# Elementwise instructions of 1024 columns over two PSUM banks, with token blocks of 256, in a chain of a Fourier filter and two feed-forward networks

## The chip, the cores and the metric

The kernel runs on one core of one Trainium2 chip. The time is the device time of one execution in microseconds; the median of three runs stands for a kernel, and one further execution is recorded by the hardware profiler. PE is the matrix engine, PEld its weight loads, DVE the vector engine, ACT the scalar engine, POOL the GpSimd engine and SP the engine that issues most DMAs. Each works through its own list of instructions in the order in which they stand and waits where a semaphore is not yet there.

## The reference

Three computations follow each other on 8 x 3072 tokens of 256 values. First a filter along the sequence, then a feed-forward network with 2048 hidden values and a piecewise activation, then a mixture of 8 experts with 1024 hidden values each, one expert a token:

```python
X = np.fft.rfft(x, axis=1)
y = np.fft.irfft(X * F, n=x.shape[1], axis=1)          # 8 batches

h = x @ w_in                                            # 24576 x 256 @ 256 x 2048
g = np.where(h >= 1, h, np.where(h <= -1, 0.0, (h + 1) ** 2 / 4))
x = g @ w_out

expert_idx = np.argmax(x @ w_gate, axis=1)
for e in range(8):
    h = np.maximum(x[mask] @ w1[e], 0.0)
    out[mask] = gate_w[mask, None] * (h @ w2[e])
```

## The kernel before

Every product of fp32 values is made of three fp16 products (high by high, high by low, low by high), so each operand of a matmul is first split into a high half and the low rest. For the hidden values the split takes ACT (high half, a rounding copy) and POOL or DVE (the rest).

The first network works on blocks of 512 tokens and slices of 128 hidden values; one step `n` is one slice of one block, 48 x 16 = 768 steps. A step has a first layer (`l1`): six matmuls of 512 columns into one bank of the pool `psH` (two buffers, tile `hps`). Then DVE clips it into `cl`, ACT squares `cl`, DVE takes the larger of the scaled `hps` and `cl` into `g`, ACT rounds `g` to `gh` and POOL computes `gl = g - gh`. Then comes the second layer (`l2`): twelve matmuls of 264 columns (256 outputs and 8 logits), four groups of 128 tokens by three products, into four accumulators `yps` of the pool `psY` (four buffers). `LAG` says how many steps the program puts the second layer behind the first. At the end of a block `finish` copies `yps` to `ysb`, and the routing (scale, `route1`, `route2`, `hilo`, `scatter`) sends its rows to the lists of the experts. All of that is in narrow DVE instructions of 4 to 32 columns.

The Fourier transform of batch 0 runs ahead of the loop, with its own choice of buffers (`ups`, `alt`), beside the conversion of the weights (`cv_...`). The transforms of batches 1 to 7 run beside the first network: a table of due times in half-steps (`ev`, `fire`) says at which place of the program each piece is written, and a scheduler then orders the instructions of each engine. Their DVE work that matters here is `al` and `yl` (the low rests of a split, line 319) and `xq` (line 412 with PSUM, line 419 from two SBUF tiles); POOL does `xs` and `xr`. `wsl` (line 713) is the low rest of the experts' weights.

The second network works on tiles of 256 tokens of one expert, two slices at a time: `m_l1` writes 2 x 256 columns into one bank, ACT makes `hh`, DVE makes `hl`, `m_l2` accumulates. Its first tiles start while the last block of the first network is still being routed.

Of the kernel before, what the change touches and what calls it, by code (L numbers as in the profile page):

```python
# [12 lines left out]
I32 = mybir.dt.int32  # L13
# [20 lines left out]
LA, LB, LC, SA, HB, SB_, LG = 3, 14, 9, 7.4, 59.8, 7.4, 5  # L34
LAG = 3
ROW = 260
# [92 lines left out]
def tile_kernel(ctx, tc, x, w_in, w_out, w_gate, w1, w2, cst, tab, fil, out):  # L129
# [37 lines left out]
    if True:  # L167
# [26 lines left out]
        def cv_run(f, i):  # L194
            if i == 0:
                k = fp.tile([128, 512], I32, tag="cl", name="cvk")
                a = fp.tile([128, 512], I32, tag="g", name="cva")
                cv[f] = (cv[f], k, a)
            raw, k, a = cv[f]
            lo, hi = raw[:, :, 0], raw[:, :, 1]  # L200
            if i == 0:
                V.tensor_scalar(a, hi, 0x7FFFFFF, 3, op0=ALU.bitwise_and, op1=ALU.logical_shift_left)
                V.tensor_scalar(k, hi, 0x7FFFFFFF, None, op0=ALU.bitwise_and)
            elif i == 1:
                V.scalar_tensor_tensor(a, lo, 29, a, op0=ALU.logical_shift_right, op1=ALU.bitwise_or)
            elif i == 2:
                V.scalar_tensor_tensor(a, hi, -(1 << 30), a, op0=ALU.bitwise_and, op1=ALU.bitwise_or)
            else:
                w = w32[f][:, 0:512]
                V.scalar_tensor_tensor(w, k.bitcast(F32), 1.125 * 2.0 ** -15, a.bitcast(F32), op0=ALU.is_ge, op1=ALU.mult)  # L210
                V.tensor_reduce(wmx[:, 0:2, f], w.rearrange("p (a b) -> p a b", a=2), axis=AX.X, op=ALU.max, apply_absolute_value=True)

        def cv_tr(f):
            tp = psH.tile([128, 512], F32, tag="h", name="hps")
            for k in range(2):
                PE.transpose(tp[:, k * 128:(k + 1) * 128], w32[f][:, 256 + k * 128:384 + k * 128], c[:, C_ID:C_ID + 128])
            cv[f] = tp

        def cv_ev(f):
            t = fp.tile([128, 256], F32, tag="gl", name="cvt", bufs=4)  # L220
            A.activation(t, cv[f][:, 0:256], AF.Copy)
            cv[f] = t

        def cv_lg(f):
            t = cv[f]
            lg = psH.tile([128, 512], F32, tag="h", name="hps")
            for k in range(2):
# [76 lines left out]
        cal = cpool.tile([128, 128], F32R, name="cal")  # L304
        bufs = {"gl": 4, "gh": 4, "wst": 3, "xi": 1, "xg": 1, "xr": 1, "ao": 1, "ag": 1, "al": 1}

# [24 lines left out]
        def ups(u):  # L331
            if u:
                return fps()
            pool, tag = ((psY, "y"), (psF, "f"), (psY, "y"))[ring[0] % 3]
            ring[0] += 1
            return pool.tile([128, 512], F32, tag=tag, name="fps")

# [171 lines left out]

        def l1(n):  # L510
            k, f = divmod(n, NF)
            xh, xl = xt[k]
            p = psH.tile([128, 512], F32, tag="h", name="hps")
            i = 0
            for kt in range(2):
                for w, xx in ((wih, xh), (wih, xl), (wil, xh)):
                    PE.matmul(p, lhsT=w[:, kt, f * 128:(f + 1) * 128], rhs=xx[:, kt, :], start=i == 0, stop=i == 5)  # L517
                    i += 1
            q = sq[k // 6]
# [5 lines left out]
        def act(n, pc):  # L525
# [9 lines left out]
        def l2(n):  # L535
            k, f = divmod(n, NF)
            gh, gl = g_t.pop(n)
            for j in range(4):
                if f == 0:
                    yps[j] = psY.tile([128, 512], F32, tag="y", name="yps")  # L540
                s = slice(j * 128, (j + 1) * 128)
                for i, (gg, w) in enumerate(((gh, woh), (gh, wol), (gl, woh))):
                    PE.matmul(yps[j][:, 0:WO], lhsT=gg[:, s], rhs=w[:, f, :], start=f == 0 and i == 0, stop=f == NF - 1 and i == 2)  # L543
            if f == NF - 1:
                finish(k, 2 * (n + LAG) + 1)

        fin = {}

        def finish(k, h):
            ysb = fp.tile([128, 4, WO], F32, tag="ysb", name="ysb")  # L550
            for j in range(4):
                if j % 2 == 0:
                    A.activation(ysb[:, j, :], yps[j][:, 0:WO], AF.Copy)
                else:
                    V.tensor_copy(ysb[:, j, :], yps[j][:, 0:WO])
            fin[k] = ysb
            o = FO if k < NBLK - 1 else (0, 0, 0, 0, 2, 2, 2, 6, 5)
# [163 lines left out]
        for f in range(CVS, NF):  # L721
            ev(CH + 2 * (f - CVS), lambda f=f: cv_split(f))
        ev(CH + 2 * (NF - CVS), wt.close)
        ev(-8, lambda: z_load(0))
# [116 lines left out]

        def m_l1(t, fpair):
# [4 lines left out]
            for i in range(2):  # L847
                f = 2 * fpair + i
# [6 lines left out]
            hh = fp.tile([128, 2, TT], F16, tag="gh", name="hh", bufs=4)  # L855
            hl = fp.tile([128, 2, TT], F16, tag="gl", name="hl", bufs=4)
            A.activation(hh, p, AF.Relu)  # L857
            V.scalar_tensor_tensor(hl, p, 0.0, hh, op0=ALU.max, op1=ALU.subtract)  # L858
            hq.append((t, fpair, hh, hl))

        yq = {}

        def m_l2():
            t, fpair, hh, hl = hq.pop(0)
            w = M["ws"][t % SLOTS]
            if fpair == 0:
                yq[t] = [psY.tile([128, 512], F32, tag="y", name="my") for _ in range(2)]
            for tk in range(2):
                s = slice(tk * 128, (tk + 1) * 128)
                for i in range(2):  # L870
                    f = 2 * fpair + i
                    wh = w[:, 4096 + f * D:4096 + (f + 1) * D]
                    wl = w[:, 6144 + f * D:6144 + (f + 1) * D]
                    for a, (hx, wx) in enumerate(((hh, wh), (hh, wl), (hl, wh))):
                        PE.matmul(yq[t][tk][:, 0:D], lhsT=hx[:, i, s], rhs=wx, start=fpair == 0 and i == 0 and a == 0,  # L875
                                  stop=fpair == 3 and i == 1 and a == 2)
            if fpair == 3:
                _, me = mst.pop(t)
# [3 lines left out]
                for tk in range(2):  # L882
                    o = fp.tile([128, D], F32, tag=("cl", "g")[tk], name="o")
                    if tk == 0:
# [7 lines left out]

        h = 2 * ((CK + 1) * NF + LAG) + 20
# [4 lines left out]
        h2 = 2 * (NS - 1 + LAG) + 1  # L898
        ev(h2 + 5, list2)
# [8 lines left out]
        for h in range(-40, 0):  # L908
            fire(h)
        for n in range(NS + 4 * NT0):  # L910
            if n < NS:
                pc = l1(n)
            else:
                m_l1(*divmod(n - NS, 4))
            fire(2 * n)
            if n < NS:
                act(n, pc)
            if n >= LAG:
                if n - LAG < NS:
                    l2(n - LAG)  # L920
                else:
                    m_l2()
                    if n == NS + LAG:
                        m_l2()
            fire(2 * n + 1)
        while hq:
            m_l2()
        order.close()

        def tail(a, b):  # L930
            for t in range(a, b):
                m_load(t)
                m_w(t)
            for n in range(4 * a, 4 * b):
                m_l1(*divmod(n, 4))
                if n > 4 * a:
                    m_l2()
            m_l2()

# [49 lines left out]
```

## Time and profile before

| | us |
|---|---|
| median of three runs | 3844.23 (3834.99 to 3852.2) |
| profiled execution, its own time | 3843.4 |
| span of that execution, first to last instruction | 3841.6 |
| busy in the span: PE / DVE / ACT / POOL | 3551.2 / 2622.7 / 2034.7 / 1747.7 |

A row of the view by groups has: line, engine, operation, what is written and read, shape (partitions x columns), count, then busy time in us and the mean length of one in ns, then the idle time of the engine just ahead of these instructions, with what ended it. A row of the timeline has start and length in us. A row of a stretch has the busy time of PE, PEld, DVE, ACT and POOL with the number of instructions, then PE's granted clock (a share of 2.4 GHz), the DMA share and GB/s. The ends of matmuls are modelled, so PE's busy share reads high.

### The profile page before, as it was taken

Reading aid. Unit: us, or ns where it says so; the run is one execution under the profiler, and the core shown is the slowest. Engines: PE = TensorE matmul, PEld = TensorE weight load, DVE = VectorE, ACT = ScalarE, POOL = GpSimd, SP = SyncE. Lnnn points to the kernel's source line nnn. Section 1 sums busy time; section 2 is a strip of 40 time slices with the busy share of each in tenths; the row PEclk is TensorE's granted clock in tenths of the full one; section 3 lists DMA queues with packets and bytes.
Section 4 is the critical chain, followed back from the end, with each engine's and each line's share of the span. In section 5 each row is a group of like instructions: output and inputs, shape, how many; then the busy total and the mean of one; then the engine's idle time right before and its main releaser. Section 6 shows DMA issues by size and latency. Waiting matters only on the chain. (4 is left out here: it accounts for less than half of the span.)

```text
span 3841.6 us, 70301 instructions
## 1 busy us (share of the span) xinstructions
PE 3551.2 (92%) x26082; PEld 2619.9 (68%) x26082; DVE 2622.7 (68%) x4808; ACT 2034.7 (53%) x3376; POOL 1747.7 (45%) x1538
## 2 busy tenths in 40 slices
PE   6888898999889889989999998999999999999998
PEld 4555665666656656656666666666688888888887
DVE  6688878887887888788689879877753333333332
ACT  5556565666666666666666666655532222222222
POOL 1355554555555555555555555545432222222222
PEclk8899999999999999999999999999999999999999
DMA  9344443433433343434334434310222222222221
GB/s 288 115 130 136 128 132 117 133 116 108 133 116 124 121 132 119 133 113 126 123 119 129 132 114 127 112 42 19 96 63 55 51 51 51 52 52 54 51 51 51
DMA packets 326124, 395.03 MB, mean 103 GB/s; under 512 B 164047, under 2 KB 254415, under 8 KB 325264
## 3 DMA queue, kind: packets, MB, share of 16 engines
q1 hardware_dynamic: 277152, 279.90, 25.6%
q0 software_dynamic: 48624, 110.58, 9.6%
q8 instruction: 207, 3.39, 0.4%
q14 instruction: 141, 1.16, 0.1%
HBM read 439.70 MB, written 120.49 MB: 146 GB/s over the span
## 5 line engine op out<-in xcount | busy, mean ns | idle before, releaser
L532 POOL TENSOR_TENSOR gl<-g,gh 128x512 f16<-128x512 f32 x768 | 925.8, 1212 | 865.0 <-ACT gh L531 810.5
L522 ACT ACTIVATE cl<-cl,sq 128x512 f32<-128x512 f32 x768 | 622.2, 811 | 398.8 <-DVE cl L521 277.7
L528 DVE SCALAR_TENSOR_TENSOR g<-hps,sq,cl 128x512 f32<-128x512 f32 x768 | 571.9, 745 | 313.2 <-ACT cl L522 290.7
L543 PE MATMUL yps<-woh,gh 128*128 128x264 f16 x3072 | 758.5, 279 | 23.4 <-ACT gh L531 12.0
L543 PE MATMUL yps<-wol,gh 128*128 128x264 f16 x3072 | 759.4, 278 | 0.0
L543 PEld LDWEIGHTS <-gh 128*128 128x128 f16 x6144 | 596.4, 99 | 233.7 <-issue 25.6
L517 PE MATMUL hps<-xh,wih 128*128 128x512 f16 x1536 | 592.0, 386 | 136.2 <-DVE g L528 128.9
L858 DVE SCALAR_TENSOR_TENSOR hl<-mh,hh 128x512 f16<-128x512 f32 x388 | 268.2, 691 | 632.8 <-ACT hh L857 632.7
L531 ACT ACTIVATE gh<-g 128x512 f16<-128x512 f32 x768 | 479.5, 626 | 401.6 <-DVE g L528 339.6
L521 DVE TENSOR_SCALAR cl<-hps,sq 128x512 f32<-128x512 f32 x768 | 614.1, 800 | 56.8 <-PE hps L517 52.7
L857 ACT ACTIVATE hh<-mh 128x512 f16<-128x512 f32 x388 | 231.4, 597 | 723.8 <-PE mh L852 721.4
L517 PE MATMUL hps<-xl,wih 128*128 128x512 f16 x1536 | 591.4, 385 | 2.7 <-DVE xl L505 2.7
L517 PE MATMUL hps<-xh,wil 128*128 128x512 f16 x1536 | 591.1, 385 | 0.0
L543 PE MATMUL yps<-woh,gl 128*128 128x264 f16 x3072 | 540.9, 278 | 37.3 <-POOL gl L532 36.1
L852 PE MATMUL mh<-xt,wslot 128*128 128x256 f16 x4656 | 571.5, 273 | 0.0
L517 PEld LDWEIGHTS <-wih 128*128 128x128 f16 x3072 | 293.5, 99 | 382.2 <-issue 181.0
L875 PE MATMUL my<-wslot,hh 128*128 128x256 f16 x3104 | 529.1, 273 | 0.0
L852 PEld LDWEIGHTS <-wslot 128*128 128x128 f16 x4656 | 455.5, 98 | 52.9
L888 POOL DMA_INDIRECT out_dram<-o,me x194 | 191.7, 988 | 659.0 <-ACT o L885 540.4
L875 PE MATMUL my<-wslot,hl 128*128 128x256 f16 x1552 | 422.9, 273 | 0.0
L543 PEld LDWEIGHTS <-gl 128*128 128x128 f16 x3072 | 285.6, 98 | 143.2 <-POOL gl L532 63.3
L875 PEld LDWEIGHTS <-hh 128*128 128x128 f16 x3104 | 303.6, 98 | 35.1
(187 smaller groups left out, 4308.0 us busy)
## 6 DMA issues: line engine op xcount, KB each, us to landing
tf<-in_fil_dram SPq DMA_DIRECT2D x113, 512.0 KB, 3.7
tt<-in_tab_dram POOLq DMA_DIRECT2D x112, 448.0 KB, 4.3
wst<-in_w_dram SPq DMA_DIRECT2D x128, 256.0 KB, 4.3
xi<-in_x_dram SPq DMA_DIRECT2D x48, 512.0 KB, 4.3
scr<-ao SPq DMA_DIRECT2D x48, 512.0 KB, 2.9
a<-scr SPq DMA_DIRECT2D x128, 192.0 KB, 2.6
scr<-z SPq DMA_DIRECT2D x128, 192.0 KB, 3.4
zt<-scr SPq DMA_DIRECT2D x48, 512.0 KB, 4.6
```

Of the source, the lines that this page charges most:

```text
L517: PE.matmul(p, lhsT=w[:, kt, f * 128:(f + 1) * 128], rhs=xx[:, kt, :], start=i == 0, stop=i == 5)
L521: V.tensor_scalar(cl, p, q[:, 5:6], q[:, 3:4], op0=ALU.max, op1=ALU.min)
L522: A.activation(cl, cl, AF.Square, bias=q[:, 11:12], scale=q[:, 4:5])
L528: V.scalar_tensor_tensor(g, p, q[:, 7:8], cl, op0=ALU.mult, op1=ALU.max)
L531: A.activation(gh, g, AF.Copy)
L532: G.tensor_tensor(gl, g, gh, op=ALU.subtract)
L543: PE.matmul(yps[j][:, 0:WO], lhsT=gg[:, s], rhs=w[:, f, :], start=f == 0 and i == 0, stop=f == NF - 1 and i == 2)
L852: PE.matmul(p[:, i, :], lhsT=w[:, wo + kt * FE + f * 128:wo + kt * FE + f * 128 + 128], rhs=xt_[:, xo + kt, :], start=a == 0, stop=a == 5)
L857: A.activation(hh, p, AF.Relu)
L858: V.scalar_tensor_tensor(hl, p, 0.0, hh, op0=ALU.max, op1=ALU.subtract)
L875: PE.matmul(yq[t][tk][:, 0:D], lhsT=hx[:, i, s], rhs=wx, start=fpair == 0 and i == 0 and a == 0, stop=fpair == 3 and i == 1 and a == 2)
L888: G.indirect_dma_start(out=out, out_offset=IOA(ap=me.bitcast(I32)[:, tk, 1:2], axis=0), in_=o, in_offset=None, bounds_check=NTOK - 1, oob_ ...
```

## The change

The step becomes a unit of four slices (`UF = 4`) of 256 tokens: 384 units in the first network, 1024 columns each. `psH` keeps two buffers, now of 1024 columns, two banks each; `psY` goes from four to two buffers, so half a block has its two accumulators at a time. The tile `g` goes away: the second DVE instruction writes back into `cl`, which has three buffers. `gh` and `gl` have three buffers of 1024 columns instead of four of 512. `LAG` goes from 3 steps to 2 units. The second layer runs over all products with `gh` first and those with `gl` last. In the second network a unit is four slices as well, two units a tile. In the transform of batch 0 the pool `psH` takes the place of every second use of `psY`. The events keep their half-steps, with four events a unit.

```diff
-LAG = 3
+LAG = 2
+UF = 4
...
-    psY = ctx.enter_context(tc.tile_pool(name="psY", bufs=4, space=bass.MemoryType.PSUM))
+    psY = ctx.enter_context(tc.tile_pool(name="psY", bufs=2, space=bass.MemoryType.PSUM))
...
-            pool, tag = ((psY, "y"), (psF, "f"), (psY, "y"))[ring[0] % 3]
+            pool, tag = ((psY, "y"), (psF, "f"), (psH, "h"))[ring[0] % 3]
...
+        def l1(n, part, p=None):
+            k, half, f0 = unit(n)
             xh, xl = xt[k]
...
+            s = slice(half * TT, (half + 1) * TT)
+            if p is None:
+                p = psH.tile([128, UF, TT], F32, tag="h", name="hps")
+            for i in range(2 * part, 2 * part + 2):
+                f = f0 + i
+                a = 0
+                for kt in range(2):
+                    for w, xx in ((wih, xh), (wih, xl), (wil, xh)):
+                        PE.matmul(p[:, i, :], lhsT=w[:, kt, f * 128:(f + 1) * 128], rhs=xx[:, kt, s], start=a == 0, stop=a == 5)
+                        a += 1
+            return p
...
-            cl = fp.tile([128, BLK], F32, tag="cl", name="cl")
+            cl = fp.tile([128, UF, TT], F32, tag="cl", name="cl", bufs=3)
             V.tensor_scalar(cl, p, q[:, 5:6], q[:, 3:4], op0=ALU.max, op1=ALU.min)
             A.activation(cl, cl, AF.Square, bias=q[:, 11:12], scale=q[:, 4:5])
...
-            g = fp.tile([128, BLK], F32, tag="g", name="g")
-            V.scalar_tensor_tensor(g, p, q[:, 7:8], cl, op0=ALU.mult, op1=ALU.max)
-            gh = fp.tile([128, BLK], F16, tag="gh", name="gh", bufs=4)
-            gl = fp.tile([128, BLK], F16, tag="gl", name="gl", bufs=4)
-            A.activation(gh, g, AF.Copy)
-            G.tensor_tensor(gl, g, gh, op=ALU.subtract)
+            V.scalar_tensor_tensor(cl, p, q[:, 7:8], cl, op0=ALU.mult, op1=ALU.max)
+            gh = fp.tile([128, UF, TT], F16, tag="gh", name="gh", bufs=3)
+            gl = fp.tile([128, UF, TT], F16, tag="gl", name="gl", bufs=3)
+            A.activation(gh, cl, AF.Copy)
+            G.tensor_tensor(gl, cl, gh, op=ALU.subtract)
...
+            todo = [(j, i, gh, w, w is woh) for j in range(2) for i in range(UF) for w in (woh, wol)]
+            todo += [(j, i, gl, woh, False) for j in range(2) for i in range(UF)]
+            for j, i, gg, w, first in todo[12 * part:12 * part + 12]:
...
-            pool, tag = ((psH, "h"), (psF, "f"))[fpair % 2]
-            p = pool.tile([128, 2, TT], F32, tag=tag, name="mh")
+                p = psH.tile([128, UF, TT], F32, tag="h", name="mh")
```

On DVE, in the part where a transform runs beside the first network, these rows stand before (line 521 is the clip, 528 the second instruction, `al` and `xq` belong to the transform, `posi` to the routing):

```order
1927 L641 TENSOR_REDUCE pos<-t 128x4
1928 L601 MEMSET oh 128x4
1929 L642 CAST posi<-pos 128x4
1930 L319 TENSOR_TENSOR al<-a_15443,ag 96x512
1931 L412 TENSOR_TENSOR xq<-fps,tf 128x512
1932 L521 TENSOR_SCALAR cl<-hps,sq 128x512
1933 L528 SCALAR_TENSOR_TENSOR g<-hps,sq,cl 128x512
1934 L713 SCALAR_TENSOR_TENSOR wsl<-wst,wsc_c,wsh 128x512
1935 L419 TENSOR_TENSOR xq<-xq,xs 128x512
1936 L528 SCALAR_TENSOR_TENSOR g<-hps,sq,cl 128x512
```

and these in the change (line 535 is the clip, 541 the second instruction, 320, 415 and 422 are the old 319, 412 and 419):

```order
1704 L508 SCALAR_TENSOR_TENSOR xl<-fps,sq,xh 128x512
1705 L535 TENSOR_SCALAR cl<-hps,sq 128x1024
1706 L541 SCALAR_TENSOR_TENSOR cl<-hps,sq,cl 128x1024
1707 L320 TENSOR_TENSOR al<-a_16610,ag 96x512
1708 L415 TENSOR_TENSOR xq<-fps,tf 128x512
1709 L422 TENSOR_TENSOR xq<-xq,xs 128x512
1710 L535 TENSOR_SCALAR cl<-hps,sq 128x1024
1711 L320 TENSOR_TENSOR yl<-xq,yh 128x512
1712 L541 SCALAR_TENSOR_TENSOR cl<-hps,sq,cl 128x1024
```

Half as many pairs of twice the width stand among the same pieces of the transform. Of the 768 pairs before, 238 have no other instruction between clip and second instruction, of the 384 pairs of the change 110.

On POOL, from the first to the second part of one transform, before (`gl` of the first network, `xr` and `xs` of the transform, `rows` the scatter of the routing):

```order
665 L319 TENSOR_TENSOR xr<-xi,xg 128x1024
666 L532 TENSOR_TENSOR gl<-g,gh 128x512 x2
667 L319 TENSOR_TENSOR xr<-xi,xg 128x1024
668 L532 TENSOR_TENSOR gl<-g,gh 128x512 x6
669 L656 DMA rows<-row,posi 198912x260
670 L532 TENSOR_TENSOR gl<-g,gh 128x512
671 L656 DMA rows<-row,posi 198912x260
672 L532 TENSOR_TENSOR gl<-g,gh 128x512
```

and in the change:

```order
415 L320 TENSOR_TENSOR xr<-xi,xg 128x1024
416 L545 TENSOR_TENSOR gl<-cl,gh 128x1024 x2
417 L320 TENSOR_TENSOR xr<-xi,xg 128x1024
418 L545 TENSOR_TENSOR gl<-cl,gh 128x1024
419 L674 DMA rows<-row,posi 198912x260
420 L545 TENSOR_TENSOR gl<-cl,gh 128x1024
421 L674 DMA rows<-row,posi 198912x260 x2
422 L545 TENSOR_TENSOR gl<-cl,gh 128x1024
```

The scatters and the pieces of the transform stand at the same places, between `gl` of twice the width. On PE each matmul of the first layer has 256 columns and a weight load of its own, and in both programs the second layer of a step or unit stands behind the first layer of the one two further, although the old program text has three.

## Rows read from the trace of the kernel before

**Rows 1.** Stretches: busy time of the engines and instruction counts, PE clock, DMA.

```profile
215.00:2480.00 2265.00, 2057.16 (x13812) 1388.87 (x13810) 1860.57 (x3319) 1444.97 (x2384) 1224.85 (x1049) 0.98 0.40 124
2480.00:2790.00 310.00, 297.51 (x2057) 199.86 (x2056) 229.42 (x505) 178.55 (x287) 154.10 (x138) 1.00 0.16 52
2790.00:3842.00 1052.00, 1036.85 (x9456) 924.50 (x9453) 383.86 (x669) 291.41 (x509) 305.06 (x302) 0.99 0.24 53
```

**Rows 2.** Groups of instructions, PE, 215 to 2480 us.

```profile
L543 PE MATMUL yps<-wol,gh 128*128 128x264 f16 x2536 | 628.9, 279 | 0.0
...
L517 PE MATMUL hps<-xh,wih 128*128 128x512 f16 x1268 | 489.0, 386 | 117.0 <-DVE g L528 115.8
```

**Rows 3.** Timeline, PE, 1500.2 to 1502.3 us.

```profile
1500.25 0.28 PE L543 MATMUL yps<-woh,gh 128*128 128x264 f16 x1
...
1501.15 0.38 PE L517 MATMUL hps<-xh,wih 128*128 128x512 f16 x1
...
1502.01 0.38 PE L517 MATMUL hps<-xl,wih 128*128 128x512 f16 x1
```

**Rows 4.** Waits of DVE, 215 to 2480 us: us in total, times, longest us.

```profile
DVE g L528 <- ACT cl L522: 207.2, 267, 3.5
...
DVE cl L521 <- PE hps L517: 38.2, 48, 2.8
```

**Rows 5.** Groups of instructions, DVE, 215 to 2480 us.

```profile
L521 DVE TENSOR_SCALAR cl<-hps,sq 128x512 f32<-128x512 f32 x634 | 506.5, 800 | 39.4 <-PE hps L517 38.2
L528 DVE SCALAR_TENSOR_TENSOR g<-hps,sq,cl 128x512 f32<-128x512 f32 x634 | 471.7, 745 | 224.1 <-ACT cl L522 207.2 <-POOL gl L532 12.4 <-ACT rs L631 1.4
L319 DVE TENSOR_TENSOR al<-a,ag 96x512 fp32r<-96x512 f32 x110 | 117.1, 1065 | 18.1 <-ACT ag L318 17.8
L319 DVE TENSOR_TENSOR yl<-xq,yh 128x512 fp32r<-128x512 f32 x110 | 116.2, 1056 | 1.8 <-ACT yh L318 1.6
L419 DVE TENSOR_TENSOR xq<-xq,xs 128x512 f32<-128x512 f32 x110 | 107.9, 981 | 17.0 <-POOL xs L413 16.6
L412 DVE TENSOR_TENSOR xq<-fps,tf 128x512 f32<-128x512 f32 x110 | 75.0, 682 | 10.2 <-ACT xs L405 9.9
...
L713 DVE SCALAR_TENSOR_TENSOR wsl<-wst,wsc_c,wsh 128x512 f16<-128x512 f32 x64 | 68.3, 1070 | 44.2 <-ACT wsh L708 41.2 <-DMA zt<-scr 2.9
...
L642 DVE CAST posi<-pos 128x4 int32<-128x4 f32 x40 | 29.7, 742 | 0.5
...
L613 DVE TENSOR_TENSOR oh<-c,m 128x32 f16<-128x32 f32 x39 | 13.0, 333 | 0.0
...
L641 DVE TENSOR_REDUCE pos<-t 128x4 f32<-128x32 f32 x40 | 6.9, 172 | 0.1
```

**Rows 6.** Tile `al` on DVE, 215 to 2480 us: lengths min/median/max in ns.

```profile
L319 DVE TENSOR_TENSOR al<-a,ag x110: 672/689/3358, 223.9 to 2472.2; 96x512 fp32r<-96x512 f32 x110
```

**Rows 7.** Timeline, 1000 to 1004.8 us.

```profile
999.57 1.15 POOL L532 TENSOR_TENSOR gl<-g,gh 128x512 f16<-128x512 f32 x1 [1.26 <-ACT gh L531]
...
1000.11 1.16 DVE L319 TENSOR_TENSOR al<-a,ag 96x512 fp32r<-96x512 f32 x1
...
1002.24 0.75 DVE L528 SCALAR_TENSOR_TENSOR g<-hps,sq,cl 128x512 f32<-128x512 f32 x1 [0.22 <-ACT cl L522]
1002.90 0.80 DVE L521 TENSOR_SCALAR cl<-hps,sq 128x512 f32<-128x512 f32 x1
```

**Rows 8.** Groups of instructions, POOL and ACT, 215 to 2480 us.

```profile
L532 POOL TENSOR_TENSOR gl<-g,gh 128x512 f16<-128x512 f32 x635 | 771.3, 1222 | 680.6 <-ACT gh L531 630.7 <-PE hps L517 36.5 <-PE yps L543 5.9
...
L522 ACT ACTIVATE cl<-cl,sq 128x512 f32<-128x512 f32 x634 | 513.5, 811 | 345.9 <-DVE cl L521 246.3 <-DVE d L602 35.6 <-DVE oh L601 25.0
...
L531 ACT ACTIVATE gh<-g 128x512 f16<-128x512 f32 x635 | 395.8, 626 | 291.2 <-DVE g L528 269.9 <-PE hps L517 4.7 <-DVE sq L255 3.8
...
L319 POOL TENSOR_TENSOR xr<-xi,xg 128x1024 fp32r<-128x1024 f32 x35 | 82.8, 2367 | 41.6 <-ACT xg L318 41.5
...
L318 ACT ACTIVATE xg<-xi 128x1024 fp32r<-128x1024 f32 x35 | 36.8, 1050 | 6.7 <-DMA xi<-in_x_dram 6.4 <-POOL gl L532 0.3
```

More of the change, by code (lines that the diff above doesn't have):

```diff
@@ L535, in l2 @@
[L535 to L539, printed above, removed]
-                    yps[j] = psY.tile([128, 512], F32, tag="y", name="yps")
[L541 to L545, printed above, removed]
@@ new lines, in act2, with l2 @@
+            gl = fp.tile([128, UF, TT], F16, tag="gl", name="gl", bufs=3)
+            A.activation(gh, cl, AF.Copy)
+            G.tensor_tensor(gl, cl, gh, op=ALU.subtract)
+            g_t[n] = (gh, gl)
+        def l2(n, part):
+            k, half, f0 = unit(n)
+            gh, gl = g_t[n]
+            if part == 0 and f0 == 0:
+                for j in range(2):
+                    yps[j] = psY.tile([128, 512], F32, tag="y", name="yps")
+            todo = [(j, i, gh, w, w is woh) for j in range(2) for i in range(UF) for w in (woh, wol)]
+            todo += [(j, i, gl, woh, False) for j in range(2) for i in range(UF)]
+            for j, i, gg, w, first in todo[12 * part:12 * part + 12]:
+                f = f0 + i
+                PE.matmul(yps[j][:, 0:WO], lhsT=gg[:, i, j * 128:(j + 1) * 128], rhs=w[:, f, :], start=f == 0 and first,
+                          stop=f == NF - 1 and gg is gl)
+            if part == 1:
+                g_t.pop(n)
+                if f0 == NF - UF:
+                    finish(k, half, 4 * (n + LAG) + 3)
@@ L557, in finish @@
+        fin = {}
+        def finish(k, half, h):
+            if half == 0:
+                fin[k] = fp.tile([128, 4, WO], F32, tag="ysb", name="ysb")
+            ysb = fin[k]
+            A.activation(ysb[:, 2 * half, :], yps[0][:, 0:WO], AF.Copy)
+            V.tensor_copy(ysb[:, 2 * half + 1, :], yps[1][:, 0:WO])
+            if half == 0:
+                return
             o = FO if k < NBLK - 1 else (0, 0, 0, 0, 2, 2, 2, 6, 5)
@@ L721, in tile_kernel @@
         for f in range(CVS, NF):
[L722 to L723 removed]
+            ev(CH + (f - CVS), lambda f=f: cv_split(f))
+        ev(CH + (NF - CVS), wt.close)
         ev(-8, lambda: z_load(0))
@@ L854, in m_l1, with m_act, m_l2 @@
                         a += 1
-            hh = fp.tile([128, 2, TT], F16, tag="gh", name="hh", bufs=4)
-            hl = fp.tile([128, 2, TT], F16, tag="gl", name="hl", bufs=4)
+            return p
+        def m_act(t, v, p):
+            hh = fp.tile([128, UF, TT], F16, tag="gh", name="hh", bufs=3)
+            hl = fp.tile([128, UF, TT], F16, tag="gl", name="hl", bufs=3)
             A.activation(hh, p, AF.Relu)
             V.scalar_tensor_tensor(hl, p, 0.0, hh, op0=ALU.max, op1=ALU.subtract)
-            hq.append((t, fpair, hh, hl))
+            hq.append((t, v, hh, hl))
         yq = {}
-        def m_l2():
-            t, fpair, hh, hl = hq.pop(0)
+        def m_l2(part):
+            t, v, hh, hl = hq[0]
             w = M["ws"][t % SLOTS]
-            if fpair == 0:
+            if v == 0 and part == 0:
                 yq[t] = [psY.tile([128, 512], F32, tag="y", name="my") for _ in range(2)]
[L868 to L877, printed above, removed]
+            todo = [(j, i, hh, wo, wo == 4096) for j in range(2) for i in range(UF) for wo in (4096, 6144)]
+            todo += [(j, i, hl, 4096, False) for j in range(2) for i in range(UF)]
+            for j, i, hx, wo, first in todo[12 * part:12 * part + 12]:
+                f = UF * v + i
+                PE.matmul(yq[t][j][:, 0:D], lhsT=hx[:, i, j * 128:(j + 1) * 128], rhs=w[:, wo + f * D:wo + (f + 1) * D],
+                          start=f == 0 and first, stop=f == 2 * UF - 1 and hx is hl)
+            if part == 1:
+                hq.pop(0)
+            if part == 1 and v == 1:
                 _, me = mst.pop(t)
@@ L909, in tile_kernel @@
             fire(h)
[L910 to L927, printed above, removed]
+        NU = NS * 2 // UF
+        for n in range(NU + 2 * NT0 + LAG):
+            mo = n - NU
+            if mo < 0:
+                p = l1(n, 0)
+            elif mo < 2 * NT0:
+                p = m_l1(*divmod(mo, 2), 0)
+            fire(4 * n)
+            if mo < 0:
+                pc = act1(n, l1(n, 1, p))
+            elif mo < 2 * NT0:
+                m_act(*divmod(mo, 2), m_l1(*divmod(mo, 2), 1, p))
+            fire(4 * n + 1)
+            if mo < 0:
+                act2(n, pc)
+            for part in range(2):
+                if n >= LAG:
+                    if n - LAG < NU:
+                        l2(n - LAG, part)
+                    else:
+                        m_l2(part)
+                if part == 0:
+                    fire(4 * n + 2)
+            fire(4 * n + 3)
         order.close()
```

64 lines of the change are left out of this document (29 added, 35 removed).

## The prediction

> **What bounds the kernel now.** I read the stretches first, then the engines inside the longest one. The kernel has three long stretches [rows 1]: 215 to 2480 us (first network beside the Fourier transforms of the later batches), 2480 to 2790 us (first network alone) and from 2790 us on (the second network). In the last one PE is busy 1036.85 of 1052 us and 9456 matmuls pass, one per 109.7 ns; nothing that ACT or DVE save there can be seen. In the first, 2265 us long, PE is busy 2057 us, DVE 1861, ACT 1445, POOL 1225.
>
> PE's busy share hides idle time, since an end is modelled: a matmul of 264 columns is written 279 ns long and one of 512 columns 386 ns [rows 2], but eight of the first take 0.90 us and four of the second 0.86 us from start to start when nothing is in the way [rows 3], 0.1125 and 0.215 each. In this stretch there are 3 x 2536 of the first and 3 x 1268 of the second: 7608 x 0.1125 = 856 us and 3804 x 0.215 = 818 us. The network alone needs 1674 of 2265 us. PE is not the limit; what it waits for at the head of a first-layer group is DVE, 115.8 us [rows 2].
>
> DVE sits idle for about 404 us there, and its own list of waits [rows 4] says that PE is hardly a reason: 38.2 us for matmuls, but 207.2 us in 267 waits for ACT's square, between the two DVE instructions of one slice. So DVE's queue, its work plus what it waits for in order, sets the pace of this stretch. The two instructions that the change merges are its largest rows, 634 each of 800 and 745 ns [rows 5].
>
> One more thing lies inside DVE's busy time. `al`, `yl` and `xq` are additions and subtractions of 512 columns with both operands in SBUF; the same instruction takes 672 ns at best, 689 in the median and 3358 at worst [rows 6], and 1065, 1056 and 981 on average [rows 5]. The timeline shows why [rows 7]: `al` starts at 1000.11 while POOL's `gl` runs from 999.57 to 1000.72, and it ends 0.55 us after that, at 1001.27: it stood until POOL was through. Over the 330 of them that is 110 x (0.393 + 0.384 + 0.309) = 119 us, for the 64 `wsl` 64 x (1.070 - 0.745) = 21 us, and for seven kinds of narrow routing instructions (from `posi`, 742 ns, to `oh`, 333 ns, the last, against 172 for the narrow `pos` that reads no such pair) about 80 us. Some 220 us of DVE's time are waits for POOL. `cl` and `g`, which read PSUM, show none (their means are their usual times).
>
> **The change part by part**, for 215 to 2480 us, where 634 slices become 317 units.
>
> *Fixed cost of DVE.* From the 32 columns of `pos` (172 ns) to the 512 of L412's `xq` (682 ns) a column costs 1.06 ns [rows 5]; 512 columns are 544 ns, so 256 ns of `cl` and 201 ns of `g` do not grow with the width. No row shows 1024 columns from two banks, so this slope stands for them. Merging saves 0.457 us a unit by durations. But the next instruction starts 0.08 to 0.09 us before the end of the one ahead: 1002.24 + 0.75 against 1002.90 [rows 7]. Back to back a merge saves 0.176 + 0.121 = 0.297 us. Where DVE waits for the square, the whole 0.256 counts. Bounds 317 x 0.297 = 94 and 317 x 0.457 = 145; I take 110, nearer the first, since most instructions do follow directly. Perfetto Trace Analysis of the Trainium skill (Optimizing Scalar/DVE Operations) gives about 125 ns of such overhead for a PSUM operand and says the profiled latency is about twice that because half overlaps; by it the estimate would be 317 x 2 x 0.125 = 79 us.
>
> *Wait for the square.* ACT's square (811 ns) becomes about 811 + 430 = 1.24 us, the slope being that of 1050 ns for 1024 columns against 626 for 512 [rows 8]. In the order, 238 of 768 pairs had nothing between `cl` and the second instruction, now 110 of 384: the same share of half as many, each 0.43 us longer. 134 waits of 0.78 + 0.43 make 162 us instead of 207 (-45); if each of the 317 units waits 0.85 it is 269 (+60). I take -25.
>
> *Slack of PE.* In both orders the second layer of a slice or unit stands behind the first layer of the one two further. Before, from the end of its first layer PE has 1.35 + 1.29 + 1.35 + 1.29 = 5.3 us of other matmuls, and the chain `cl`, square, `g`, `gh` takes 0.80 + 0.81 + 0.75 + 0.63 = 3.0 us [rows 5, 8]: 2.3 us to spare. After, PE has 10.6 us (24 x 0.1125 and 24 x 0.1097, twice each) and the chain takes 1.34 + 1.24 + 1.29 + 1.05 = 4.9 us: 5.7 us to spare. For `gl` it is 1.8 us of further matmuls, since all `gh` come first, against 2.3 us on POOL. What disturbs the chain (routing, the transforms) does not grow, so PE falls behind less often and DVE's 38 us of waiting for it shrink: -30, bounds -38 and 0. The cover for this is that depth of two units; without it each late `gl` would show at once.
>
> *Lock with POOL.* `gl` of 1024 columns should take about as long as `xr`, 2.37 us for 1024 [rows 8]; I take 2.3 for two times 1.22. POOL's share for it stays near 771/2265 = 0.34, but what arrives while it runs waits half of 2.3 instead of half of 1.22. A random arrival pays 0.33 x 1.15 = 0.38 us instead of 0.34 x 0.61 = 0.21: 394 wide instructions x 0.17 = 67 us more. The narrow ones come in chains, where one wait lets the others through: 0 to 64 more, I take 25. In all +90, bounds 0 (the wait hides one for the square) and +220 (all double).
>
> *First layer in 256 columns.* Twice the matmuls: 7608 x 0.1097 = 835 against 818 us, 17 us more on PE, covered by PE's 208 us of idle time. ACT and POOL only get shorter; neither is the limit. Evictions of `yps` come twice as often with half the tiles: the same count.
>
> *Elsewhere.* From 2480 to 2790 us PE idles 12.5 us; I take -8 (0 to -12). In the second network PE has 2.6 us of second layer and 2.6 of first layer before it needs a bank pair again, and an ACT and a DVE eviction take at most 2 x (0.63 + 0.75) = 2.8 us [rows 5, 8]: nothing. At the start some 15 tiles of the first batch now share the two buffers of the weight preparation: if each waits for one ACT copy, 15 x 0.63 = 9 us; I take +3, since not all of them will have to. Loads and routing stay at the same half-steps, but for two.
>
> *Sum.* -110 - 25 - 30 + 90 - 8 + 3 = -80. The profiled execution took 3843.4 us (span 3841.6), 0.8 from the median of the three runs, 3844.2, so I read it as the median: **3763 us**.
>
> **Rivals.** *The lock is worth less* (0.15): if the waits for POOL fall where DVE would wait for the square anyway, the +90 goes: 3763 - 90 = 3673. For it: both waits sit between the same two instructions. Against it: the second instruction often follows directly, with nothing between that could be blocked.
>
> *The lock doubles, slower* (0.18): with +220 and the square unchanged the sum is -110 - 30 + 220 - 5 = +75 (the 5 are the -8 and +3 of the other stretches): 3918 us. It decides from the point where the waits for POOL grow by more than about 145 us, from 220 to 365. For it: the wide instructions already wait 0.36 us on average, 1.7 times what a random arrival at `gl` would. Against: half as many `gl` can block only half as often. SBUF — State Buffer of the Trainium skill (Who interferes with whom) states the rule: an exclusive hold, for the whole instruction, between POOL and a DVE instruction with two SBUF inputs. The trace agrees with it (3358 ns against 672).
>
> *Longer instructions, later results* (0.12, no change): if what PE and ACT wait for is the end of the longer instruction, every wait grows with the width and eats the fixed cost: the square's goes to 207 + 60, -110 + 60 + 90 - 30 - 5 = +5, about 3848. Perfetto Trace Analysis (same section) advises just that, breaking instructions up where an engine is not saturated but makes others wait. DVE's 0.82 speaks for it, the 5.7 us of slack against.
>
> The forecast has 0.55 (3700 to 3824). **Range 3650 to 3870:** below lies little but a lost lock with the larger bounds of the fixed cost, above the rest of the slower case. A difference of 0.5%, 19 us, is about what these runs can tell. Faster 0.55 + 0.15 = 0.70, same 0.12, slower 0.18.
>
> **What would show it.** Clip and second instruction near 1.34 and 1.29 us, square 1.24, `gl` 2.2 to 2.4. DVE's waits for the square 160 to 200 us. PE's waits for DVE at the head of a first-layer group well under 115.8. `al`, `yl`, `xq` with means near 1.25 us and a longer tail. The stretch to about 2480 us ending some 80 us earlier, the last one unchanged near 1050 us. Wrong it would be if `al` and its kind average over 1.5 us, if the square's wait grows past 260, or if PE turns out to wait for `gl`.

## The result and the profile after

The change makes the kernel faster: 3741.0 us (median of 4 runs, 3736.4 to 3755.5) against 3848.1 for the kernel before beside it, ratio 0.9734 [0.9697, 0.977]. The forecast was 3763 us.

Three marks cut both profiled executions into the same stretches: the start of the first first-layer matmul, the start of the last transform matmul, the start of the last second-layer matmul of the first network.

| stretch, us | before | after | difference |
|---|---|---|---|
| until the first network starts | 131.3 | 138.8 | +7.5 |
| first network beside the transforms | 2374.0 | 2268.2 | -105.8 |
| first network alone | 310.0 | 304.8 | -5.2 |
| second network | 1026.3 | 1026.4 | +0.1 |

The gain lies beside the transforms. The stretches of the changed kernel, cut as in [rows 1]:

```profile
215.00:2382.00 2167.00, 2036.58 (x17641) 1762.16 (x17641) 1772.59 (x2702) 1292.61 (x1754) 1162.69 (x732) 0.99 0.43 130
2382.00:2687.00 305.00, 296.19 (x2684) 261.44 (x2682) 224.91 (x402) 151.48 (x183) 144.50 (x85) 1.00 0.17 54
2687.00:3738.00 1051.00, 1035.99 (x9486) 927.43 (x9484) 328.10 (x465) 255.48 (x306) 303.59 (x299) 0.99 0.23 53
```

DVE's busy time fell from 1860.57 to 1772.59 us and the stretch from 2265 to 2167. That looks like cause and effect; e2 below shows that it is not. PE's busy time hardly moved, 2057.16 to 2036.58 us: it stood idle for 208 us of the stretch before and for 130 after. DVE by groups, 215 to 2382 us (to [rows 5]):

```profile
L535 DVE TENSOR_SCALAR cl<-hps,sq 128x1024 f32<-128x1024 f32 x318 | 424.8, 1336 | 65.0 <-PE hps L528 61.3 <-PE fps L647 3.4
L541 DVE SCALAR_TENSOR_TENSOR cl<-hps,sq,cl 128x1024 f32<-128x1024 f32 x318 | 406.6, 1279 | 151.6 <-ACT cl L536 149.3 <-issue 0.7
L320 DVE TENSOR_TENSOR al<-a,ag 96x512 fp32r<-96x512 f32 x111 | 135.0, 1216 | 21.7 <-ACT ag L319 21.7
L422 DVE TENSOR_TENSOR xq<-xq,xs 128x512 f32<-128x512 f32 x110 | 111.6, 1015 | 19.4 <-POOL xs L416 17.8
L320 DVE TENSOR_TENSOR yl<-xq,yh 128x512 fp32r<-128x512 f32 x109 | 109.4, 1003 | 0.5 <-ACT yh L319 0.5
...
L731 DVE SCALAR_TENSOR_TENSOR wsl<-wst,wsc_c,wsh 128x512 f16<-128x512 f32 x64 | 63.5, 996 | 44.4 <-ACT wsh L726 38.7 <-issue 5.5
...
L660 DVE CAST posi<-pos 128x4 int32<-128x4 f32 x40 | 11.8, 294 | 0.5
```

Clip and second instruction are as long as forecast (1336 and 1279 ns). `al` is longer than before (1216 against 1065), `xq` hardly, `yl`, `wsl` and above all `posi` are shorter. POOL and ACT in the same stretch (to [rows 8]):

```profile
L545 POOL TENSOR_TENSOR gl<-cl,gh 128x1024 f16<-128x1024 f32 x318 | 695.1, 2186 | 551.0 <-ACT gh L544 267.8 <-issue 211.7 <-ACT rs L649 44.4
...
L536 ACT ACTIVATE cl<-cl,sq 128x1024 f32<-128x1024 f32 x318 | 394.4, 1240 | 400.8 <-DVE cl L535 369.3 <-DVE eq L627 7.9 <-DVE sm L601 7.8
```

DVE's own waits (to [rows 4]):

```profile
DVE cl L541 <- ACT cl L536: 149.3, 138, 2.9
DVE cl L535 <- PE hps L528: 61.3, 45, 3.3
```

The square's wait fell from 207.2 us, but the wait for PE's matmuls, which was to shrink, rose from 38.2. PE's own waits:

```profile
PE fps L328 <- ACT yh L319: 55.7, 46, 3.2
PE fps L328 <- DVE yl L320: 18.6, 25, 1.9
PE fps L645 <- DVE oh L631: 16.6, 14, 3.4
...
PE hps L528 <- DVE cl L541: 0.7, 1, 0.7
```

The wait of the first layer for a free `hps`, 115.8 us before [rows 2], is 0.7 us. What is left of PE's standing is mostly at the matmuls of the transforms (L328), for `yh` and `yl`. That is not what the clip waits for, though: in 40 of its 45 waits PE had not stood at a transform matmul in the 8 us before, and for 52 of the 61 us it was at work on first-layer matmuls (my own sums over the records). DVE had caught up with a PE that was at work.

### The profile page after: what moved, and what is told of

Its sections match the earlier page's. It is cut to its first block, busy times and chain, and to the rows that moved or that the text cites. A ratio compares the mean times of both kernels' runs of the same rounds, so it can differ in the third digit from the quotient of the medians.

```text
span 3738.2 us, 75215 instructions
## 1 busy us (share of the span) xinstructions
PE 3528.7 (94%) x30690; PEld 3071.6 (82%) x30690; DVE 2464.9 (66%) x3846; ACT 1810.0 (48%) x2414; POOL 1672.0 (45%) x1154
## 5 line engine op out<-in xcount | busy, mean ns | idle before, releaser
L545 POOL TENSOR_TENSOR gl<-cl,gh 128x1024 f16<-128x1024 f32 x384 | 837.2, 2181 | 673.8 <-ACT gh L544 326.0
L528 PE MATMUL hps<-xh,wih 128*128 128x256 f16 x3072 | 841.8, 274 | 7.7 <-ACT xh L507 5.5
L528 PE MATMUL hps<-xl,wih 128*128 128x256 f16 x3072 | 841.2, 274 | 2.5 <-DVE sq L256 2.5
L528 PE MATMUL hps<-xh,wil 128*128 128x256 f16 x3072 | 840.7, 274 | 0.0
L536 ACT ACTIVATE cl<-cl,sq 128x1024 f32<-128x1024 f32 x384 | 476.3, 1240 | 497.8 <-DVE cl L535 460.1
L528 PEld LDWEIGHTS <-wih 128*128 128x128 f16 x6144 | 596.2, 98 | 89.6 <-issue 10.1
L541 DVE SCALAR_TENSOR_TENSOR cl<-hps,sq,cl 128x1024 f32<-128x1024 f32 x384 | 491.1, 1279 | 197.1 <-ACT cl L536 194.6
L535 DVE TENSOR_SCALAR cl<-hps,sq 128x1024 f32<-128x1024 f32 x384 | 513.3, 1337 | 111.0 <-PE hps L528 105.6
L544 ACT ACTIVATE gh<-cl 128x1024 f16<-128x1024 f32 x384 | 405.4, 1056 | 311.9 <-DVE cl L541 306.5
L878 ACT ACTIVATE hh<-mh 128x1024 f16<-128x1024 f32 x194 | 198.6, 1024 | 653.4 <-PE mh L870 461.5
L528 PEld LDWEIGHTS <-wil 128*128 128x128 f16 x3072 | 301.9, 98 | 40.0 <-issue 2.8
```

The lines of the kernel that those rows point to most:

```text
L528: PE.matmul(p[:, i, :], lhsT=w[:, kt, f * 128:(f + 1) * 128], rhs=xx[:, kt, s], start=a == 0, stop=a == 5)
L541: V.scalar_tensor_tensor(cl, p, q[:, 7:8], cl, op0=ALU.mult, op1=ALU.max)
L544: A.activation(gh, cl, AF.Copy)
L545: G.tensor_tensor(gl, cl, gh, op=ALU.subtract)
```

## The experiments

Each is an edit of the changed kernel. Ratios are to the kernel before, run on the same chip. Besides the ratio I read two numbers from each trace: the transform stretch between the first two marks, and DVE's held time in it. This is, for every DVE instruction, its length beyond that which a tenth of its kind (line, operation, tile, shape) stays below, summed. An instruction that stands for POOL is long for its kind, so the held time measures the waits that no list of waits shows. It is my own sum over the records, good to a few us. Stretch and held time come from one profiled execution each. e4 and e7 change next to nothing in the text of that stretch and yet move it by 14 and 13 us, so differences of that size are not read.

| kernel | ratio [95%] | transform stretch, us | held, us |
|---|---|---|---|
| before | 1 | 2374.0 | 273 |
| the change | 0.9734 [0.9697, 0.977] | 2268.2 | 290 |
| e1_all_512 | 0.9711 [0.9691, 0.9731] | 2239.8 | 270 |
| e2_dve_512 | 0.9732 [0.9711, 0.9753] | 2270.7 | 282 |
| e3_pool_512 | 0.9647 [0.9625, 0.9669] | 2230.3 | 239 |
| e4_second_512 | 0.9762 [0.974, 0.9784] | 2282.2 | 299 |
| e5_pool_quarter | 0.9347 [0.9327, 0.9366] | 2129.2 | 75 |
| e6_inverse_later | 0.9763 [0.9736, 0.979] | 2265.7 | 288 |
| e7_start_ring | 0.9748 [0.9732, 0.9765] | 2281.2 | 295 |
| e8_four_banks | 0.9665 [0.9643, 0.9687] | 2243.1 | 225 |
| e9_two_banks | 0.9947 [0.9928, 0.9965] | 2328.7 | 228 |
| e10_gl_between | 0.9749 [0.9719, 0.9779] | 2267.9 | 297 |
| e11_pool_256 | 0.9596 [0.958, 0.9612] | 2200.5 | 192 |
| e12_pool_all_256 | 0.9564 [0.9538, 0.959] | 2213.5 | 193 |

**The width of the instructions.** e1 takes all five elementwise instructions of a unit back to 512 columns, e2 the two of DVE alone, e3 the one of POOL alone; units, buffers and PE's work stay.

```diff
-            V.tensor_scalar(cl, p, q[:, 5:6], q[:, 3:4], op0=ALU.max, op1=ALU.min)
+            for b in (slice(0, 2), slice(2, 4)):                                      # e1, e2
+                V.tensor_scalar(cl[:, b], p[:, b], q[:, 5:6], q[:, 3:4], op0=ALU.max, op1=ALU.min)
...
-            G.tensor_tensor(gl, cl, gh, op=ALU.subtract)
+            for b in (slice(0, 2), slice(2, 4)):                                      # e1, e3
+                G.tensor_tensor(gl[:, b], cl[:, b], gh[:, b], op=ALU.subtract)
```

> The change with its units, banks and order of matmuls, but every elementwise instruction of the first network (clip, square, second instruction, gh, gl) made as two of 512 columns. Theory of the fixed cost: DVE gets back about 0.31 us a unit, 332 units beside the transforms, some 100 us, less what finer steps save of the wait for the square (159 us now): 3800 to 3845 us, a ratio to before of 0.985 to 1.0. Rival, the depth: what counts is that PE now runs two units of 1024 columns ahead instead of two of 512, whatever the width of an instruction: 3735 to 3765 us, 0.970 to 0.978.

> Only the two DVE instructions of the first network are made as two of 512 columns; ACT and POOL keep 1024. Fixed cost: 3820 to 3850 us, since the whole saving of DVE is undone and the square still starts after the second half. Depth: 3735 to 3765 us.

> Only POOL's gl is made as two of 512 columns; DVE and ACT keep 1024. If DVE's waits for POOL grow with the length of one POOL instruction, as the term of +90 had it, the mean of al, yl and xq falls from 1.07 to about 1.0 us and the time by 20 to 60 us, to 3680 to 3720. If a POOL that follows itself at once keeps DVE out as long as one long instruction, or the waits are few enough, no change: 3735 to 3750 us.

With everything narrow again (e1) the gain of the change is still there: 0.9711 against 0.9734. So the width of all five together is not where it came from. e2 shows it for DVE alone. Its stretch (137 to 2407 us) and its two groups:

```profile
137.00:2407.00 2270.00, 2130.57 (x18394) 1835.07 (x18393) 1927.38 (x3467) 1346.99 (x1833) 1209.61 (x755) 0.99 0.41 129
```

```profile
L536 DVE TENSOR_SCALAR cl<-hps,sq 128x512 f32<-128x512 f32 x664 | 506.2, 801 | 70.7 <-PE hps L528 66.9 <-POOL gl L547 3.4
...
L543 DVE SCALAR_TENSOR_TENSOR cl<-hps,sq,cl 128x512 f32<-128x512 f32 x662 | 465.1, 743 | 148.3 <-ACT cl L537 144.0 <-issue 2.7
```

and the same stretch of the changed kernel (139 to 2407 us):

```profile
139.00:2407.00 2268.00, 2127.39 (x18388) 1837.66 (x18387) 1841.24 (x2804) 1351.04 (x1833) 1210.39 (x755) 0.99 0.42 129
```

DVE is busy 86 us more in e2 (1927.38 against 1841.24) and the stretch is as long. DVE's idle time took all of it: 343 us instead of 427. The fixed cost that the merge saves is real, and beside a POOL at 1024 columns it is worth nothing that these runs can tell. The square's wait tells as little. In e1 (135 to 2375 us):

```profile
DVE cl L536 <- PE hps L528: 111.6, 68, 5.8
...
DVE cl L544 <- ACT cl L538: 37.3, 123, 2.6
```

The time is within 0.3% of the change's: much of what DVE no longer waits for the square it waits for PE.

POOL's width does count. With `gl` alone in 512 columns (e3) the ratio falls to 0.9647, though PE, ACT and the two large DVE instructions do what they did in the change. The groups of `gl` and `al` in e3 (142 to 2372 us):

```profile
L546 POOL TENSOR_TENSOR gl<-cl,gh 128x512 f16<-128x512 f32 x662 | 797.2, 1227 | 533.0 <-issue 261.1 <-ACT gh L544 227.4 <-ACT rs L650 42.7
...
L320 DVE TENSOR_TENSOR al<-a,ag 96x512 fp32r<-96x512 f32 x112 | 114.4, 1022 | 21.5 <-ACT ag L319 21.5
```

e3 and e1 differ in the width on DVE and ACT alone, with POOL narrow in both, and there the wide form is faster: 0.9647 against 0.9711, intervals apart, 22 us by the medians (3701.6 against 3723.7). So the width of DVE and ACT is not worth nothing everywhere. The held time is 31 us less in e3 too; no run tells that from the fixed cost.

**The banks.** e8 has units of two slices, so every elementwise instruction of the first network has 512 columns and one bank, and four buffers of one bank each: the same four banks as the change. e9 is the same program text with two such buffers, two banks as in the kernel before.

```diff
-LAG = 2
-UF = 4
+LAG = 4
+UF = 2
...
-    psH = ctx.enter_context(tc.tile_pool(name="psH", bufs=2, space=bass.MemoryType.PSUM))
+    psH = ctx.enter_context(tc.tile_pool(name="psH", bufs=4, space=bass.MemoryType.PSUM))    # e8 only
...
-            cl = fp.tile([128, UF, TT], F32, tag="cl", name="cl", bufs=3)
+            cl = fp.tile([128, UF, TT], F32, tag="cl", name="cl", bufs=6)
```

> Units of two slices of 256 tokens, so 512 columns in every elementwise instruction of both networks, as before the change; but four one-bank buffers hold the first layer's output where the change has two of two banks, and clip, gh and gl have six buffers of 512 columns. Two tiles of the first transform use another tag, for space. If the gain is PE's run-ahead, four banks of it whatever the width: 3700 to 3745 us, ratio 0.965 to 0.977. If it is the width of the instructions: 3800 us or more.

> The same kernel with two one-bank buffers for the first layer's output, two banks left empty: the run-ahead of the kernel before, with the token blocks of the change. Run-ahead: 3815 to 3860 us, ratio 0.995 to 1.005, and PE's waits for DVE at the head of a first-layer group back over 100 us. If blocks of 256 tokens, the deeper buffers in SBUF or the order of the second layer made the gain, it stays under 3760 us.

Four banks of narrow instructions give 0.9665, two banks 0.9947. This one number, how many banks the first layer may fill ahead, is worth 110 us by the medians (3819.1 to 3709.2). In the profiled executions 86 us of it lie in the transform stretch, 12 in an earlier start of the first network and 8 in the first network alone. With two banks the second layer stands 1024 columns behind the first layer in PE's order, as in the kernel before, with four banks 2048, as in the change. PE's waits in e9, 143 to 2471 us:

```profile
PE hps L528 <- DVE cl L541: 105.7, 99, 5.3
PE yps L558 <- POOL gl L545: 33.2, 40, 3.4
PE fps L328 <- ACT yh L319: 8.9, 10, 1.7
```

and in e8, 131 to 2374 us:

```profile
PE fps L328 <- ACT yh L319: 42.0, 33, 4.1
PE fps L328 <- DVE yl L320: 16.3, 24, 1.9
...
PE hps L528 <- DVE cl L541: 2.0, 2, 1.5
```

e9 waits where the kernel before waits (115.8 us for `hps`, [rows 2]), e8 where the change does. The stretches of e9 and e8:

```profile
143.00:2471.00 2328.00, 2141.36 (x18327) 1822.67 (x18326) 1885.59 (x3455) 1510.95 (x2490) 1281.49 (x1083) 0.98 0.40 126
131.00:2374.00 2243.00, 2130.37 (x18392) 1839.57 (x18391) 1887.14 (x3469) 1513.14 (x2497) 1292.97 (x1087) 0.99 0.42 131
```

DVE, ACT and POOL have the same work in both. PE's idle time falls from 187 to 113 us, 74 of the 85 us.

**POOL.** e5 computes `gl` for the first of each unit's four slices only, and all four products with `gl` read that one. It leaves out three quarters of the low halves of the hidden values; PE has as many matmuls. e11 keeps the whole of `gl` and takes it in four instructions of 256 columns; e12 cuts `xr` and `xs` into 256 columns as well.

```diff
-            G.tensor_tensor(gl, cl, gh, op=ALU.subtract)
+            G.tensor_tensor(gl[:, 0], cl[:, 0], gh[:, 0], op=ALU.subtract)            # e5
...
+            for b in range(UF):                                                       # e11, e12
+                G.tensor_tensor(gl[:, b], cl[:, b], gh[:, b], op=ALU.subtract)
...
-                G.tensor_tensor(xs, xs, tf[:, :, D:], op=ALU.mult)
+                for b in range(2):                                                    # e12
+                    G.tensor_tensor(xs[:, b], xs[:, b], tf[:, b, D:], op=ALU.mult)
```

> gl is computed for the first of four slices alone and all products with gl read that slice, so three quarters of gl are left out and the output is not the reference's; PE does the same work. POOL's largest instruction shrinks from 2.18 to about 0.6 us. If the waits for POOL cost time in proportion, al, yl and xq fall to about 0.8 us, DVE gains some 150 us of work and the time falls by 50 to 110 us, to 3620 to 3680. If PE and its waits for the transforms set the pace: 3690 to 3730 us.

> The change with gl as four POOL instructions of 256 columns, DVE and ACT at 1024. If DVE's waits for POOL go with the length of one POOL instruction, they fall below those at 512 columns (242 us in the long stretch, 290 at 1024) to about 200, and the time to 3670 to 3700 us, ratio 0.957 to 0.965. If POOL's own fixed cost (some 0.27 us an instruction) makes gl late, it rises above that at 512: 3710 to 3760 us.

> This takes gl in four instructions of 256 columns and cuts POOL's two instructions of the transforms in the same way: xr of 1024 columns into four, xs of 512 into two. If what costs time is how long POOL keeps DVE standing at one instruction, the waits of al, xq and yl fall a little further than with gl alone in 256 (mean of al 891 ns there): al 800 to 870, in all some 25 us less of such waits, and the time is 10 to 25 us below that kernel: 3650 to 3670 us, ratio 0.953 to 0.958. The rival: POOL pays its fixed cost some 300 more times (about 0.2 us each, 64 us), and xs, for which DVE's xq already waits, comes later by one fixed cost; then DVE's waits for xs grow and the time is 3680 to 3700 us, ratio 0.960 to 0.965.

The groups of `gl` and `al` in e5 (136 to 2265 us), and then in e11 (134 to 2334 us):

```profile
L545 POOL TENSOR_TENSOR gl<-cl,gh 128x256 f16<-128x256 f32 x331 | 238.9, 722 | 619.5 <-ACT gh L544 298.4 <-issue 231.4 <-ACT rs L649 40.7
...
L320 DVE TENSOR_TENSOR al<-a,ag 96x512 fp32r<-96x512 f32 x112 | 86.3, 771 | 29.0 <-ACT ag L319 28.6
```

```profile
L546 POOL TENSOR_TENSOR gl<-cl,gh 128x256 f16<-128x256 f32 x1324 | 917.5, 727 | 430.4 <-ACT gh L544 194.3 <-issue 188.6 <-ACT rs L650 46.1
...
L320 DVE TENSOR_TENSOR al<-a,ag 96x512 fp32r<-96x512 f32 x112 | 99.7, 891 | 15.3 <-ACT ag L319 15.3
```

In e11 POOL is busier with `gl` than in the change, 917.5 against 722.8 us, and the kernel is 1.4% faster. What counts is not POOL's load but how long one of its instructions keeps DVE standing. That PE gets its `gl` sooner is not the reason: PE and its weight loads wait for `gl` for 1.3 us in the change, 1.1 in e3 and 3.1 in e11. Over `gl` in 1024, 512 and 256 columns and the quarter of it the held time is 290, 239, 192 and 75 us and the stretch 2268, 2230, 2200 and 2129 us: (2268 - 2129) / (290 - 75) = 0.65 us of time for one held. e5 cuts POOL's load as well, and gained more than forecast (3591 us against 3620 to 3680); without it the slope is (2268 - 2200) / (290 - 192) = 0.69. e12 holds DVE as long as e11 (193 against 192), and its ratio lies beside e11's with overlapping intervals: neither the further gain nor the loss can be seen. These two are the fastest whole kernels of the study, 1.4 and 1.7% below the change.

**Other suspects.** e6 writes the inverse transform's matmuls later, so that `yh` is there. e10 puts the products with `gl` back among the others. e4 takes the second network's two instructions back to 512 columns, e7 the pool `psH` out of the first batch's transform.

```diff
-LA, LB, LC, SA, HB, SB_, LG = 3, 14, 9, 7.4, 59.8, 7.4, 5
+LA, LB, LC, SA, HB, SB_, LG = 3, 14, 9, 7.4, 59.8, 7.2, 8                              # e6
...
+            todo = [(j, i, gg, w, w is woh and gg is gh) for i in range(UF) for j in range(2) for gg, w in ((gh, woh), (gh, wol), (gl, woh))]   # e10
...
+            for b in (slice(0, 2), slice(2, 4)):                                      # e4
+                A.activation(hh[:, b], p[:, b], AF.Relu)
+                V.scalar_tensor_tensor(hl[:, b], p[:, b], 0.0, hh[:, b], op0=ALU.max, op1=ALU.subtract)
...
-            pool, tag = ((psY, "y"), (psF, "f"), (psH, "h"))[ring[0] % 3]
+            pool, tag = ((psY, "y"), (psF, "f"))[ring[0] % 2]                         # e7
```

> The change with the inverse transform written 8 half-steps behind the forward one instead of 5 (and the pieces 7.2 apart instead of 7.4, so that the last one keeps its place). If PE, which now waits 57 + 75 us for yh at the head of an inverse transform, is held up there, those waits fall by half and the time by 20 to 50 us, to 3685 to 3720. If PE's waits there only show that DVE's work is late, they move to another place: 3725 to 3745 us.

> The change with the second layer's products in the old order, each gl directly behind its gh products, instead of all gl last. If the later place of gl makes the gain, PE's waits for gl come back (32 + 57 us before) and the time rises by 20 to 60 us, to 3755 to 3795. If the run-ahead covers gl anyway: 3728 to 3745 us.

> Only the second network goes back to two instructions of 512 columns on ACT and DVE. By the prediction nothing, since PE is busy from end to end there: 3735 to 3747 us, the last 1026 us unchanged within 2. Rival, the wider evictions hold a bank pair long enough to matter: 10 us or more either way.

> The change with the transform of batch 0 in psY and psF in turn, without psH. The first matmul of the first layer starts at 138.8 us in the change, 131.3 before. If the shared pool of the weight preparation costs the 7 us: 130 to 134 us, time 5 to 8 us less. If the smaller psY costs them, or the closer weight splits do, the start stays at 137 us or later and the time within 5 us.

None of the four can be told from the change. In e6 the wait moved; PE's waits, 138 to 2404 us:

```profile
PE fps L328 <- DMA tt<-in_tab_dram: 37.2, 19, 3.4
PE fps L328 <- ACT yh L319: 15.8, 15, 3.4
```

`yh` is waited for 15.8 us instead of 57.5, and the matmuls wait for their table instead. e10 shows that the order of the products is no part of the gain. In e4 the second network takes 1026.8 us, the same with twice as many evictions. In e7 the first network starts at 130.4 us and the time is the same; over all these kernels that start lies between 130 and 143 us without a pattern that I can read, so the +7.5 of the result is not explained.

## Why the prediction held, and which of its steps did not

The time, the sign and the stretch were right: -106 us beside the transforms where -75 stood (-110 - 25 - 30 + 90), -5 alone where -8 stood, nothing in the second network. The way there was not: that the sum came so near is luck, since a term far too large and one far too small made up for each other. From kernel to kernel the transform stretch goes: before to e9, 2374.0 to 2328.7 (-45); e9 to e8, the banks (-86); e8 to e3, units of four slices with DVE and ACT wide (-13, which is within what equal programs differ); e3 to the change, POOL's width (+38).

**"So DVE's queue, its work plus what it waits for in order, sets the pace of this stretch": this step failed.** Its term, the fixed cost, stood at -110 (94 to 145). The durations saved what was foreseen, but e2 puts 86 us of work back on DVE at an unchanged time, and e1 to e3 gives -22 us for the widths of DVE and ACT together, with POOL narrow and the square's wait included. Perfetto Trace Analysis of the Trainium skill (Optimizing Scalar/DVE Operations) says that grouping into larger operations can help throughput if the engine is saturated. The trace agrees by the condition: DVE was busy 1841 of 2268 us in the change, 81%, and e2 shows that this was not saturated.

The step ahead of it, "PE is not the limit", was wrong as well. The 1674 us are the matmuls of the network alone; those of the transforms and the routing, beside it on PE, were left out. By the records, with their modelled ends, PE was busy 2057.16 of 2265 us [rows 1], 91%. From kernel to kernel the stretch differs above all by PE's idle time (the stretch, its marks rounded to 1 us, less PE's busy time): 221 us before, 187 in e9, 141 in the change, 118 in e1, 113 in e8, 108 in e3, 89 in e11, 42 in e5. PE's busy time goes only from 2153 to 2087 us over the same kernels.

**"Slack of PE": the mechanism was right, the size too small.** It stood at -30, with DVE's 38 us of waiting for PE [rows 4] as the bound. e9 against e8 measures -86 in the stretch. The better bound was the 115.8 us in [rows 2]: PE waited for DVE to free `hps`, while DVE waited for PE and for the square. Neither was quite full (PE busy 2057, DVE 1861 of 2265 us); with two banks each delay of the one reached the other. The prediction had read that row and set it aside because PE "is not the limit". And the 38 us did not shrink but rose to 61: freed of `hps`, DVE more often caught up with a PE that was at work. Why it is more than before is not shown. It may be the pair of banks, which the clip has only when 24 matmuls are through: e8, with single banks, has 38.6 us (131 to 2374 us), the change 78.5 (139 to 2407 us).

**"Lock with POOL": right in kind and sign, too large.** +90 stood for it; +38 is what 1024 columns cost against 512 (e3 to the change), between the forecast's +90 and the nothing of the rival "the lock is worth less". Of 336 `al`, `yl` and `xq` 118 are held for more than 0.1 us before, 1.00 us on average, and 97 after, 1.36 us. The longer hold was foreseen; that fewer instructions meet one was not: 131 of them start under a POOL instruction before, 102 after. So the average over all 336 went from 0.36 to 0.40 us, not to the 0.53 that +0.17 would have made. The narrow instructions, for which 25 us more were taken, are held 110 us in all against 103 (the held time of the table, kinds of 4 to 32 columns): `posi` fell from 742 to 294 ns, others rose. SBUF — State Buffer of the Trainium skill (Who interferes with whom) states that the second of the two blocks until the first is through; e3, e11 and e5 agree, since shorter or fewer POOL instructions shorten `al` (1211, 1022, 891, 771 ns).

**"Wait for the square"**: -25 stood, about -58 came (207.2 to 149.3 us), and in e1, with three quarters of it gone, the time is within 0.3% of the change's, DVE waiting for PE instead.

**Not foreseen: -45 us from before to e9**, with 512 columns and two banks in both. What the two differ in is the token block, the two accumulators, the deeper `cl`, `gh` and `gl`, and the order that comes of it. The whole time gains less, about 20 us (0.9947), since the first network starts 11 us later in e9. The held time fell by as much as the stretch, 273 to 228, but I made no kernel that takes these parts one by one, so which of them it is stays open.

Open as well: why a microsecond that POOL holds DVE costs 0.65 while 86 us of DVE's own work (e2) cost nothing. A guess, not shown: the work of the merged pairs comes evenly, into gaps that DVE has anyway, and the holds come up to 3.5 us at once on `al`, `xq` and `yl`, whose results PE waits for (its wait for `yh` falls along: 57.5, 41.8, 35.6, 13.8 us in the order of the POOL series). e6 does not settle it: that wait went without gain, but a wait for the table came in its place.

## What to carry to other kernels

Add up all the work of an engine, the side work too, before you call it no limit: here PE was busy for 91% of the stretch, and most of what the kernels won was its idle time. When two engines each wait for the other in one stretch and neither is quite full, price a deeper buffer between them by the larger of the two waits before pricing any instruction's fixed cost: in this one case the banks gave 86 us where halving the count of DVE's two large instructions gave nothing beside a wide POOL. The width of an instruction is a choice for each engine: wide is no loss on DVE and ACT here (a gain of 22 us where POOL is narrow), and on POOL, beside a DVE that reads two SBUF tiles, four short instructions beat a long one by 1.4% although POOL is busier. A right total proves no term: -110 for a cost worth 0 to -22 and -30 for one worth -86 summed to nearly the measured time.

## What the runs showed of the hardware that was not expected

A held DVE instruction can be kept out by several POOL instructions in a row. The timeline of the changed kernel, 1008 to 1014 us (POOL and DVE; start and length in us):

```profile
1008.00 1.00 POOL L674 DMA_INDIRECT rows<-row,posi  x1 [1.42 <-DMA rows<-row,posi]
...
1008.86 4.09 DVE L320 TENSOR_TENSOR al<-a,ag 96x512 fp32r<-96x512 f32 x1
...
1009.01 2.16 POOL L545 TENSOR_TENSOR gl<-cl,gh 128x1024 f16<-128x1024 f32 x1
...
1011.11 1.29 POOL L416 TENSOR_TENSOR xs<-xs,tf 128x512 f32<-128x512 f32 x1
...
1012.88 1.33 DVE L535 TENSOR_SCALAR cl<-hps,sq 128x1024 f32<-128x1024 f32 x1
```

`al` starts while POOL issues a scatter, and `gl` 0.15 us after it; it ends at 1012.95, 0.55 us after the end of `xs` at 1012.40: it stood for both, and `xs` followed `gl` without a gap. In e11 it is the same even with pieces: one `al` of 4.57 us, from 646.62 us on, outlasts an `xs` and four `gl` of 256 columns. There most get in at the next boundary, though: of the 102 that are held, 82 outlast at most one POOL instruction, and the mean hold is 0.61 us.
